# Loading the first seven row tiles for the norms into a buffer of the weight conversions

## The chip, the cores and the metric

The kernel runs on one core of a Trainium2 chip. The metric is the device time in microseconds, the median of several runs. The engines are named as the profile names them: PE is TensorE, which multiplies matrices, and PEld its weight load; DVE is VectorE; ACT is ScalarE; POOL is GpSimd; SP is SyncE, which in this kernel only issues transfers (DMAs). A `q` behind an engine's name (SPq) is the queue of transfers that this engine issues.

## The reference, cut to what matters

Attention with positive random features, and a gated feed-forward layer behind it, all in float32:

```python
# q, k, v: (8, 8, 576, 64); omega: (128, 64)
def phi(x):
    proj = np.einsum('bhsd,md->bhsm', x, omega)
    sq = np.sum(x * x, axis=-1, keepdims=True) / 2.0
    h = proj - sq
    h = h - np.max(h, axis=-1, keepdims=True)
    return np.exp(h) / np.sqrt(m)
q_p, k_p = phi(q * scale), phi(k * scale)
kv  = np.einsum('bhsm,bhsd->bhmd', k_p, v)
z   = np.sum(k_p, axis=2)
out = np.einsum('bhsm,bhmd->bhsd', q_p, kv) / (np.einsum('bhsm,bhm->bhs', q_p, z)[..., None] + 1e-06)
# x: (4608, 512), the heads side by side
y = (1 / (1 + np.exp(-(x @ w_gate))) * (x @ w_val)) @ w_out
```

The weights come as float64: they are converted on the chip. `sq`, the sum of the squares of each row of q and k in each head, is what this document calls the norms.

## The kernel before, in words

The 8 batches are worked as four units `u` of two batches, so a unit has 1152 rows, nine tiles of 128 rows. Each unit falls into two halves `b`, because of the batch limit in the middle of the fifth tile, and into four pairs of heads `p`.

Work is written as Python generators that are stepped in turn. `attention` (L681) keeps up to six of them active and takes one step of each in turn: for each unit and half one `norms` task for k and one for q (one norms task at a time), four `keys` tasks (two at a time) and four `queries` tasks. The first unit starts with the first two key tasks and the norms of k; the norms of q follow when those of k are done.

- `norms` (L493): for each row tile it loads 128 rows of all heads (128 x 512, 256 KB, L499) into a tile `nat`, of which there are three, squares it on ACT into `x2` (L501), and sums each head's 64 squares on DVE into `ss` (L503). When all tiles of the half are through, one small DVE instruction scales the sums into `sq` (L507). In the first half of a unit k has five row tiles and q four; in the second half it is the other way about.
- `projected` (L513): loads k or q the other way round (`raw`, L519), waits until `sq` of its unit and half is there, splits each group of row tiles into a high part (ACT, L70) and a low part (POOL, L71), and multiplies both by omega in three matmuls each (PE, L547 to L549, the result in `pp`). DVE takes the maximum (L552) and joins it with `sq` (L556).
- `keys` (L561): loads v (L571), works out the bias `nb` (DVE, L574), takes the exponent of each tile and head (ACT, L587), multiplies by v (PE, L595, `pkv`) and copies the result out (ACT, L600, `kv`). One key task has ten exponents, which are computed tile by tile with both heads in turn, while the matmuls go through all five tiles of the first head and then of the second. A product of this line shows as two matmuls in the trace, so one task has twenty.
- `queries` (L604) follows with transposes, exponents and products, and stores x, transposed, to memory.

Beside that, weights are converted: `first_weights` (L153) takes the four tiles `e0` to `e3`, `convert_weights` (L166) fourteen tiles `c0` to `c13`. Each is a tile of 128 x 3584 words with the tag `cv`, of which there are two: four parts take the raw float64 words (two loads of 512 KB, L144), two the result, one is scratch. A conversion is six DVE instructions (L78 to L94) and one POOL instruction (L96) for each half. A step of `first_weights` is taken with every 32nd step of the attention (L725). When the first 256 columns of x are through, the first pass of the feed-forward layer (`gv`, L247) is mixed in; later come the second pass (`gw`, L351) and the output product (`po`, L465).

A tile with a tag and a number of buffers waits for the tile that used its buffer before: the fourth `nat` load waits until the first `nat` has been squared, and so on. The order of the instructions in each engine's list is fixed when the program is built, from the order of the code and from when a planner takes each to be ready; on the chip each list runs in order, so an instruction that waits holds up all that stand behind it in its list. That counts for SP's list of transfers too.

Of the kernel before, what the change touches and what calls it, by code (L numbers as in the profile page):

```python
# [9 lines left out]
F32 = mybir.dt.float32  # L10
# [4 lines left out]
U32 = mybir.dt.uint32  # L15
# [3 lines left out]
DM = H * D  # L19
DF = 1536  # L20
P = 128
# [21 lines left out]
WP = 512  # L43
# [56 lines left out]
def attn_glu_kernel(ctx: ExitStack, tc, qT, kT, qn, kn, va, om, ident, w, out):  # L100
# [382 lines left out]
        yield  # L483

    sqs, kvs, kmid = {}, {}, {}
    through = [0] * NP

    def span(name, b):

        g = GROUPS[name][b]  # L490
        return g[0][0], g[-1][-1] + 1

    def norms(pool, name, u, b, src):  # L493

        t0, t1 = span(name, b)
        s = pool.tile([P, MID + 1, H], F32, tag="ss", bufs=2, name=f"ss{name}{u}_{b}")[:, : t1 - t0]
        for t in range(t0, t1):
            x = pool.tile([P, DM], F32, tag="nat", bufs=3, name=f"nat{name}{u}_{t}")
            nc.sync.dma_start(out=x, in_=src[u, :, t, :])  # L499
            x2 = pool.tile([P, DM], F32, tag="x2", bufs=2, name=f"x2{name}{u}_{t}")  # L500
            nc.scalar.activation(out=x2, in_=x, func=AF.Square)  # L501
            yield
            nc.vector.tensor_reduce(  # L503
                out=s[:, t - t0, :], in_=x2.rearrange("p (h d) -> p h d", d=D), axis=AX.X, op=ALU.add
            )
        sq = pool.tile([P, MID + 1, H], F32, tag="sq", bufs=6, name=f"sq{name}{u}_{b}")
        nc.vector.tensor_scalar(  # L507
            out=sq[:, : t1 - t0], in0=s, scalar1=SCALE * SCALE / 2.0, scalar2=None, op0=ALU.mult
        )
        sqs[name, u, b] = sq  # L510
        yield
# [158 lines left out]
    for u in range(U):  # L670
        for b in range(2):
            for n, x in (("k", kn), ("q", qn)):
                for p in range(NP):
                    if p == 1:
                        tasks.append((("n" + n, u, b), (), lambda pool, a=(n, u, b, x): norms(pool, *a)))
                    needs = (("k", u, p, b - 1),) if n == "k" and b else (("k", u, p, b), ("q", u - 1 + b, p, 1 - b)) if n == "q" else ()
                    make = keys if n == "k" else queries
                    tasks.append(((n, u, p, b), needs, lambda pool, a=(u, p, b), f=make: f(pool, *a)))
# [32 lines left out]
    with tc.tile_pool(name="early", bufs=1) as early:  # L711
        gates = first_pass()
        with tc.tile_pool(name="a", bufs=1, side="right") as pool:
# [7 lines left out]
            n = 0  # L721
# [7 lines left out]
            n = credit = 0  # L729
# [16 lines left out]
        for n, _ in enumerate(gates):  # L746
# [6 lines left out]
            if n == left - 2 * NE:  # L753
                parts = operands(0)
                x = next(parts)
# [110 lines left out]
```

## Time and profile before

| | us |
|---|---|
| median of 3 runs | 1237.84 (1237.4 to 1239.83) |
| the profiled execution, its own time | 1239.43 |
| span of the profile | 1237.6 |
| mean granted TensorE clock | 0.968 |

| engine | busy us | share of the span |
|---|---|---|
| PE | 1172.3 | 95% |
| DVE | 864.5 | 70% |
| POOL | 542.7 | 44% |
| ACT | 530.7 | 43% |

Row of a timeline: start in us from the start of the span, duration in us, engine, line of the code, operation, output tile <- input tiles, shapes, how many instructions are merged in the row, and in square brackets how long the engine had been idle before and what released it. Transfers stand there with the time at which SP issued them, not with the time at which the data landed. Row of a view by windows: the stretch, its length, the busy time of each engine with the number of its instructions, the granted TensorE clock (1.00 is full speed), the busy share of the 16 DMA engines and the rate. Row of a view of transfers: name, queue, number, size, and the median time in us from issue to landing.

The attention with the weight conversions and the first pass fills the first 590 us; after that PE runs the second pass and the output product almost without a gap.

### The profile page before, as it was taken

The page shows a single profiled execution, that of the slowest core. Times are in us where ns is not written, and L with a number is a line of the kernel's source. Part 1 is how long each engine was busy: PE and PEld are TensorE (multiplying, and loading weights), DVE is VectorE, ACT ScalarE, POOL GpSimd, SP SyncE. Part 2 cuts the span into 40 slices and gives each one's busy share as a digit, 9 for nine tenths or more (in the row PEclk, how much of TensorE's full clock was granted, in tenths as well). Part 3 has the DMA queues.
Part 4 walks back from the last instruction along what each step waited for, and adds up shares of the span by engine and source line. Part 5 has one row for each costly group of instructions (what it writes and reads, how often), then busy time and mean ns, then how long its engine had stood idle before and what let it go on. Part 6 is the DMA issues. An engine that isn't in the chain of part 4 may idle for free.

```text
span 1237.6 us, 23990 instructions
## 1 busy us (share of the span) xinstructions
PE 1172.3 (95%) x8828; PEld 1109.8 (90%) x8828; DVE 864.5 (70%) x1907; ACT 530.7 (43%) x1164; POOL 542.7 (44%) x599
## 2 busy tenths in 40 slices
PE   6798989999898999899899999999998899999998
PEld 5788978798887888788899999999998899999998
DVE  4889888999698866433566656666569777777773
ACT  5556755565455463342423322232325344343331
POOL 2454365556457552131466666666666211111110
PEclk7798989999899999899899999999999999999999
DMA  7667767786657641461432333323337676666662
GB/s 247 213 199 228 210 219 253 238 268 237 226 182 252 223 153 39 139 202 52 152 128 106 123 135 124 121 93 125 124 135 267 203 226 195 188 191 189 198 191 94
DMA packets 104950, 219.43 MB, mean 177 GB/s; under 512 B 11136, under 2 KB 42112, under 8 KB 103040
## 3 DMA queue, kind: packets, MB, share of 16 engines
q1 hardware_dynamic: 87984, 198.94, 48.5%
q10 hardware_dynamic: 16848, 18.95, 4.4%
q8 instruction: 70, 1.15, 0.4%
q14 instruction: 48, 0.39, 0.1%
HBM read 141.82 MB, written 76.02 MB: 176 GB/s over the span
## 4 chain that ended last, share of the span: by engine, by line
PE 71%; DVE 12%; issue 7%; DMA 5%; POOL 3%; ACT 1%; SPq 1%; ACTq 0%; DVEq 0%; POOLq 0%
PE gw L351 27%; PE po L465 20%; PE gv L247 10%; PE pkv L595 4%; PE pnq L638 4%; PE ptq L626 2%; DVE mxq L552 2%; DVE hq L615 1%; DMA xr<-xT 1%; DMA xT<-xsq 1%; DMA rawk<-kT 1%; POOL loq L71 1%; DVE hmq L556 1%; PE ppk L547 1%; POOL xe L71 1%
## 5 line engine op out<-in xcount | busy, mean ns | idle before, releaser
L351 PE MATMUL gw<-xl,u 128*128 128x256 f32 x3024 | 364.6, 283 | 6.9 <-ACT p L362 3.6
L351 PEld LDWEIGHTS gw<-xl,u 128*128 128x128 f32 x3024 | 363.5, 191 | 7.9 <-DVE u L331 3.9
L465 PE MATMUL po<-u,yh 128*128 128x256 f32 x1512 | 272.4, 283 | 0.0
L465 PEld LDWEIGHTS po<-u,yh 128*128 128x128 f32 x1512 | 234.8, 191 | 0.0
L465 PE MATMUL po<-u,yl 128*128 128x256 f32 x756 | 214.0, 283 | 3.3 <-DVE yl L71 3.3
L247 PE MATMUL gv<-xe,wh 128*128 128x512 f32 (+1 forms) x640 | 201.0, 388 | 2.1 <-POOL xe L71 2.1
L70 ACT ACTIVATE yh<-yr 128x896 fp32r<-128x896 f32 x108 | 100.2, 950 | 156.8 <-PE po L465 86.3
L465 PEld LDWEIGHTS po<-u,yl 128*128 128x128 f32 x756 | 144.3, 191 | 3.9 <-DVE yl L71 3.9
L247 PEld LDWEIGHTS gv<-xe,wh 128*128 128x128 f32 x640 | 117.3, 194 | 20.1 <-POOL xe L71 4.5
L71 POOL TENSOR_TENSOR yl<-yr,yh 128x896 fp32r<-128x896 f32 x17 | 38.0, 2232 | 215.3 <-PE po L465 139.9
L247 PE MATMUL gv<-xe,wl 128*128 128x512 f32 (+1 forms) x320 | 125.8, 394 | 2.7 <-POOL wl L71 1.6
L71 DVE TENSOR_TENSOR yl<-yr,yh 128x896 fp32r<-128x896 f32 x91 | 103.0, 1144 | 31.5 <-PE po L465 19.1
L331 DVE TENSOR_TENSOR u<-gw,p 128x256 f32<-128x256 f32 x144 | 60.7, 422 | 59.2 <-PE gw L351 51.1
L595 PE MATMUL pkv<-v,kpk 128*128 128x66 f32 x512 | 84.4, 290 | 13.3 <-ACT kpk L587 12.6
L595 PEld LDWEIGHTS pkv<-v,kpk 128*128 128x128 f32 x512 | 77.0, 209 | 21.5 <-ACT kpk L587 19.8
L71 POOL TENSOR_TENSOR lok<-rawk,hik 128x256 fp32r<-128x256 f32 (+1 forms) x80 | 55.5, 712 | 68.0 <-ACT hik L70 67.6
L456 DVE TENSOR_TENSOR yr<-yr 128x128 f32<-128x128 f32 x144 | 60.1, 451 | 35.3 <-DMA yr<-ye 34.8
L71 POOL TENSOR_TENSOR xe<-xr,xe 128x512 fp32r<-128x512 f32 (+1 forms) x40 | 49.1, 1244 | 74.2 <-ACT xe L70 62.4
L71 POOL TENSOR_TENSOR loq<-rawq,hiq 128x256 fp32r<-128x256 f32 (+1 forms) x80 | 56.5, 718 | 55.5 <-ACT hiq L70 54.7
L587 ACT ACTIVATE kpk<-ppk,nb 128x128 f32<-128x128 f32 x256 | 69.8, 393 | 17.4 <-DVE nb L574 17.1
L638 PEld LDWEIGHTS pnq<-kv,qpq 128*128 128x128 f32 (+1 forms) x640 | 70.5, 189 | 6.5 <-ACT qpq L628 4.3
L638 PE MATMUL pnq<-kv,qpq 128*128 128x66 f32 (+1 forms) x640 | 74.9, 273 | 1.4 <-ACT qpq L628 1.2
(108 smaller groups left out, 2166.6 us busy)
## 6 DMA issues: line engine op xcount, KB each, us to landing
yl<-yl SPq DMA_DIRECT2D x36, 896.0 KB, 3.8
yr<-yl SPq DMA_DIRECT2D x72, 448.0 KB, 3.5
xr<-xT SPq DMA_DIRECT2D x68, 256.0 KB, 4.7
c<-w SPq DMA_DIRECT2D x28, 512.0 KB, 5.1
w<-c SPq DMA_DIRECT2D x14, 1024.0 KB, 4.5
v<-va SPq DMA_DIRECT2D x32, 330.0 KB, 3.4
natk<-kn SPq DMA_DIRECT2D x36, 256.0 KB, 4.2
natq<-qn SPq DMA_DIRECT2D x36, 256.0 KB, 3.9
```

Of the source, the lines that this page charges most:

```text
L70: nc.scalar.activation(out=hi, in_=x, func=AF.Copy)
L71: (lo_engine or nc.vector).tensor_tensor(out=lo, in0=x, in1=hi.bitcast(F32), op=ALU.subtract)
L247: nc.tensor.matmul(gv, lhsT=u[:, s], rhs=v, start=(m == 0), stop=(m == 3 * KC - 1))
L331: return nc.vector.tensor_tensor(out=o, in0=a, in1=b, op=ALU.add)
L351: nc.tensor.matmul(o, lhsT=u[:, k, s], rhs=v[:, kc, :], start=(first and m == 0), stop=(m == 5), skip_group_check=not first,)
L456: nc.vector.tensor_tensor(out=raw[:, o], in0=raw[:, a], in1=raw[:, b], op=op)
L465: nc.tensor.matmul(o, lhsT=u[:, i, :], rhs=v[:, k, :], start=(j + m == 0 and n in (1, 6, 5, 4)), stop=(j == NPAIR - 1 and m == 2), skip_gr ...
L552: nc.vector.tensor_reduce(out=m.rearrange("p t h -> p (t h)"), in_=pp, axis=AX.X, op=ALU.max)
L587: nc.scalar.activation(out=kp[t][:, h, :], in_=pp[:, 2 * i + h, :], func=AF.Exp, bias=nb[:, t - t0, h : h + 1], scale=SCALE,)
L595: nc.tensor.matmul(pkv[:, h, :], lhsT=kp[b * MID + i][:, h, :], rhs=v[:, i, h, :], start=(i == 0), stop=(i == MID),)
L626: nc.tensor.transpose(out=pt[:, i, :], in_=h_sb[:, i, :], identity=id_sb)
L638: nc.tensor.matmul(pn[r, 2 * i + h, :], lhsT=qp[:, 2 * i + h, r], rhs=kvs[u, p, bb][:, h, :], start=True, stop=True,)
```

## The change

The first seven loads of `norms` (the five k tiles and the first two q tiles of the first half of the first unit) go to seven parts, of 2 KB in each partition, of one tile of the tag `cv`, which has just room for seven. So none of them waits for a `nat` buffer to come free. All later row tiles use the three `nat` buffers as before. Since that tile takes the first of the two `cv` buffers, `e0` takes the second and `e1` the first, once the seven tiles in it have been squared; before, `e0` and `e1` found both free.

```diff
     sqs, kvs, kmid = {}, {}, {}
+    firsts = []
     through = [0] * NP
...
         for t in range(t0, t1):
-            x = pool.tile([P, DM], F32, tag="nat", bufs=3, name=f"nat{name}{u}_{t}")
+            if not firsts:
+                firsts.append(pool.tile([P, 7 * WP], U32, tag="cv", bufs=2, name="nats").bitcast(F32))
+            if u == 0 and b == 0 and len(firsts) < 8:
+                n = len(firsts) - 1
+                firsts.append(firsts[0][:, n * DM : (n + 1) * DM])
+                x = firsts[-1]
+            else:
+                x = pool.tile([P, DM], F32, tag="nat", bufs=3, name=f"nat{name}{u}_{t}")
             nc.sync.dma_start(out=x, in_=src[u, :, t, :])
```

## The prediction

> **What bounds the kernel now.** I read the page first, then, since the change touches only the first 16 us, the timeline of each engine there, the landing times of the transfers, and the windows for rate and clock.
>
> ```profile
> span 1237.6 us, 23990 instructions
> PE   6798989999898999899899999999998899999998
> PEclk7798989999899999899899999999999999999999
> ```
>
> Each digit is a fortieth of the span, 30.9 us. PE is the bound nearly everywhere, but its first digit is 6 and the clock granted to it there 7: the opening is a chain of waits, and it is the only stretch that the change can shorten directly. From the 20th digit on PE is full, so what the attention saves earlier comes off the end.
>
> SP's list in the opening (start, duration, how many are merged), then landing times of single row tiles, v and the first q tiles (last number: us from issue to landing):
>
> ```profile
> 1.65 0.42 SPq L499 DMA_DIRECT2D natk<-kn x1
> 2.58 4.83 SPq L499 DMA_DIRECT2D natk<-kn x3
> 7.46 0.43 SPq L571 DMA_DIRECT2D v<-va x1
> 8.69 0.33 SPq L499 DMA_DIRECT2D natk<-kn x1
> 9.06 0.43 SPq L571 DMA_DIRECT2D v<-va x1
> 9.59 4.31 SPq L499 DMA_DIRECT2D natq<-qn x3
> 16.32 0.91 SPq L144 DMA_DIRECT2D e<-w x2
> ```
>
> ```profile
> natk<-kn SPq DMA_DIRECT2D x1, 256.0 KB, 5.3
> ```
>
> ```profile
> v<-va SPq DMA_DIRECT2D x1, 330.0 KB, 3.3
> natk<-kn SPq DMA_DIRECT2D x1, 256.0 KB, 2.8
> ```
>
> ```profile
> natk<-kn SPq DMA_DIRECT2D x1, 256.0 KB, 4.1
> ```
>
> ```profile
> natq<-qn SPq DMA_DIRECT2D x3, 256.0 KB, 4.4
> ```
>
> The row at 2.58 holds three issues in 4.83 us; one alone takes 0.42. So two went out at once and the fourth row tile only near 7.1, when the first had been squared; the fifth went out at 8.69, and three q tiles needed 4.31 us. Landing is issue plus the last number: the third k tile about 3.0 + 5.3 = 8.3, the fourth 7.1 + 2.8 = 9.9, the fifth 8.69 + 4.1 = 12.8.
>
> What those landings hold up, on ACT, DVE and PE:
>
> ```profile
> 12.91 0.63 ACT L501 ACTIVATE x2k<-natk 128x512 f32<-128x512 f32 x1 [2.10 <-DMA natk<-kn]
> 14.44 1.28 ACT L501 ACTIVATE x2q<-natq 128x512 f32<-128x512 f32 x2 [0.90 <-DMA natq<-qn]
> 16.66 2.18 ACT L587 ACTIVATE kpk<-ppk,nb 128x128 f32<-128x128 f32 x8 [0.95 <-DVE nb L574]
> 19.18 2.24 ACT L587 ACTIVATE kpk<-ppk,nb 128x128 f32<-128x128 f32 x8
> 26.28 0.28 ACT L600 ACTIVATE kv<-pkv 128x132 f32<-128x132 f32 x1 [2.95 <-PE pkv L595]
> 26.46 1.52 ACT L70 ACTIVATE hik<-rawk 128x256 fp32r<-128x256 f32 x5
> ```
>
> ```profile
> 10.65 0.69 DVE L503 TENSOR_REDUCE ssk<-x2k 128x8 f32<-128x512 f32 x1 [0.44 <-ACT x2k L501]
> 13.57 0.69 DVE L503 TENSOR_REDUCE ssk<-x2k 128x8 f32<-128x512 f32 x1 [1.64 <-ACT x2k L501]
> 14.18 0.68 DVE L552 TENSOR_REDUCE mxk<-ppk 128x4 f32<-128x512 f32 x1
> 15.87 0.68 DVE L552 TENSOR_REDUCE mxk<-ppk 128x4 f32<-128x512 f32 x1
> 16.47 0.16 DVE L574 SCALAR_TENSOR_TENSOR nb<-sqk,hmk 128x10 f32<-128x10 f32 x1
> 22.45 0.43 DVE L78 TENSOR_SCALAR e<-e 128x512 uint32<-128x512 uint32 x1 [4.15 <-DMA e<-w]
> ```
>
> ```profile
> 8.49 0.58 PE L547 MATMUL ppk<-omH,lok 128*128 128x256 f32 x1 [8.49 <-POOL lok L71]
> 14.21 0.41 PE L549 MATMUL ppk<-omH,hik 128*128 128x256 f32 x1
> 14.79 0.28 PE L549 MATMUL ppk<-omH,hik 128*128 128x256 f32 x1
> 17.08 2.25 PE L595 MATMUL pkv<-v,kpk 128*128 128x66 f32 x8 [2.01 <-ACT kpk L587]
> 27.72 0.58 PE L547 MATMUL ppk<-omH,lok 128*128 128x256 f32 x1 [1.48 <-POOL lok L71]
> ```
>
> The fifth k tile lands at 12.8, its square ends at 13.54, its sum at 14.26, and only behind that does DVE get to the maximum at 14.18, to two more and to that of 15.87; the bias of the first key task (16.47) follows, its exponents start at 16.66, and PE, done with projections at 14.79 + 0.28 = 15.07, starts again at 17.08 after 2.01 us without work. Everything behind hangs on it in order: the second kv at 26.28, the next split at 26.46, the next projection at 27.72.
>
> **The change part by part.** *SP.* SP issued the first three tiles 0.47 apart (1.65, then 2.58 with one transfer between). Without the waits the fourth and fifth go out at about 3.5 and 4.0. v, v and the three q tiles follow at that pace from 4.4 to 6.3 instead of 7.46 to 13.9. No instruction is added, no transfer either; the byte count is the same.
>
> *Landing.* What had been held back by SP now stands behind other bytes:
>
> ```profile
> 6.00:8.00 2.00, 0.00 (x0) 0.00 (x0) 0.69 (x1) 1.41 (x4) 0.28 (x1) 1.00 0.65 250
> 8.00:10.00 2.00, 1.51 (x7) 1.51 (x8) 1.17 (x2) 1.81 (x6) 2.00 (x4) 1.00 0.87 287
> 10.00:12.00 2.00, 2.00 (x11) 2.00 (x11) 1.49 (x3) 0.81 (x2) 1.35 (x3) 1.00 0.89 262
> 12.00:14.00 2.00, 2.00 (x12) 2.00 (x11) 0.43 (x1) 0.63 (x1) 0.00 (x0) 1.00 0.81 302
> ```
>
> The last two numbers are the DMA engines' share and GB/s. The transfers are nearly busy already, 250 to 302 GB/s, with only 0.65 at 6 to 8. A tile of 256 KB (0.262 MB) takes 0.262 / 0.27 = 1.0 us at such a rate, so behind the third tile (8.3) the fourth lands at 9.3 and the fifth at 10.3. Bounds: 9.3 if the rate has slack, 12.8 if the bytes set it and nothing moves; I take 10.3, since row tiles so far landed in the order of issue, and the share of 0.65 leaves room. Then v, v and two q tiles, 2 x 0.338 + 2 x 0.262 = 1.2 MB at 282 (mean of the last two rows) need 4.25 us: the second q tile lands at 14.5, and its square ends at 14.5 + 0.64 = 15.15. ACT has both q squares ahead of the exponents (14.44, then 16.66).
>
> *The bias.* The sum of the fifth k tile now ends at about 10.3 + 0.63 + 0.69 = 11.6, say 12.2 with a maximum in between; it is late no more. Late next is PE's projection: the maximum of the row 15.87 needs the matmul that starts at 14.21 and ends at 14.62, and DVE's list has it ahead of the bias, although it belongs to the second key task. So that maximum runs from 14.65 to 15.25, where it ran from 15.87 to 16.47, and the exponents start at 15.45 (16.66 less 1.22), just behind the q squares' 15.15. **Gain 1.2 us**: 2.6 us earlier norms are worth less than half, since the projection and the q squares come next.
>
> *Clock and the products behind.* PE's gap shrinks from 2.01 to about 0.8 us. What the clock makes of that:
>
> ```profile
> 14.65:18.06 3.41, 1.29 (x7) 1.00 0.93 291
> 21.47:24.89 3.42, 3.42 (x18) 0.50 1.00 385
> ```
>
> (Stretch, length, PE busy, clock, DMA share, rate.) A stretch of 3.41 us with 1.29 us of work was followed by half speed, and a stretch full of `pkv`, 18 in 3.42 us, 0.19 us each, stayed at half. So a busy PE is not enough: these short products do not bring the speed back. In the changed kernel the stretch to 18.06 holds two projections and some ten products that wait for exponents; I take half speed from 18.06 as now, and the gain stays 1.2 us. The Trainium skill ("TensorE: Matmul & The Clock Gate", the table of the two states) has the clock fall only after at least one idle window of about 3.4 us; the trace disagrees, since it fell here after an idle time of 2.01 us. By this page of the Trainium skill the smaller gap would leave full speed; what this gives is the rival below.
>
> *The buffers.* e0 moves to the other `cv` buffer and costs nothing. e1 waits for the second q square, about 15.2, and today e0 itself is issued only at 16.32, with e1 behind it: nothing. If the code called for e1 earlier, it would wait on SP with all loads behind it; that cover is the 16.32. In the later rotation every tile waits for the same predecessor as before: e2 for e0, as now. The `nat` rotation likewise, save for the first tiles of the next half, which find free buffers.
>
> *e0's load.* It stands ten issues of 0.47 behind the fifth k tile's 4.0, plus 0.5, so it may go out at 9.2 instead of 16.32. With the same bytes ahead of it, it lands at best the slack of the DMA engines earlier: (1 - 0.65) x 2.0 + (1 - 0.81) x 2.0 = 1.1 us. DVE waited 4.15 us for it and had time; nothing.
>
> Sum against the profiled execution (1239.43, span 1237.6): 1.2 us off, a span of 1236.4. The median of the runs is 1.6 below that execution, so the forecast is 1237.84 - 1.2 = **1236.6**. A shift of the opening also moves all work against the clock's steps of 3.41 us: a stretch more or less at half speed costs up to 1.7 us, and one or two of those either way make the scatter of this case, 1236.6 within 2.6.
>
> **The rivals.** *The clock stays up* (or DVE's list is put in another order, with the first bias ahead of the second task's maximum, so that the products begin at 15.07 and are dense). Then the second task's first pass ends with its exponents, 15.45 + 2 x 2.52 (the distance of 16.66 and 19.18) = 20.5, and ten products at half of 0.19 end at 21.5; the second kv comes 4.8 us earlier than 26.28: **1233.0**. For: the gap is less than half. Against: the two rows above, full of such products and still at half. 0.20.
>
> *e0's conversion stands ahead of the first bias* (slower). DVE's list is made anew, and e0's load moves up seven us in SP's. If its first DVE step (22.45, which waits for the landing) comes to stand before the bias, the exponents start at 22.45 + 0.43 + 0.16 = 23.0 instead of 16.66, 6.4 later: **1244.2**. It decides from the point where that one step passes the bias; standing behind it, it costs nothing. For: e0 does move up, and the list is not just the code's order (a load of v stands at 7.46 ahead of the fifth k tile). Against: today both biases and two sums stand between. 0.14.
>
> *The bytes bind and nothing gets earlier*: the fifth tile still lands near 12.8, or the second q tile, only now behind both v, lands as late as today, and its square holds the exponents. Gain about 0: **1237.8**. For: shares of 0.87 and 0.89. Against: the 0.65. 0.16.
>
> **How the numbers follow.** The forecast has 0.50. A measurement of this kernel can tell about 0.2% (2.5 us; three runs spread over 2.4). Faster by more: 0.16 of the forecast's own scatter, 0.19 of the clock rival, 0.03 of the bytes rival, 0.38. Slower: 0.03 of the forecast, 0.13 of e0's rival, 0.03 of the bytes', 0.19. Within: the rest, 0.43. The range goes from 1231.0, the clock rival with one more stretch at full speed, to 1241.5, the forecast's scatter and the lower side of e0's; most of e0's case (0.12) and the lowest of the clock's (0.06) are left out.
>
> **What would show it.** In SP's list five row tiles in a row by 4.5 us, with no wait; the fifth k square near 10.4 rather than 12.91; the first exponent near 15.4; PE's gap under 1 us; second kv near 25. Wrong: a first exponent before 14 or after 16.6, full speed from 18 to 25, or DVE waiting for e0 ahead of the first bias. If the opening gains 1.2 and the end does not, the gain was given back later.

## The result, and the profile after

| | before | after |
|---|---|---|
| median of 11 runs, us | 1239.37 (1232.04 to 1242.72) | 1245.34 (1242.12 to 1252.72) |
| ratio, 95% interval | | **1.0066** (1.0047 to 1.0084) |
| the profiled execution, its own time | 1239.43 | 1245.34 |
| its span | 1237.6 | 1243.5 |

The change made the kernel 0.7% slower (by the two medians 6 us are lost, by the ratio 8), where 1.2 us were forecast as won. Lines of `after` stand 8 higher than the same lines of before (L501 is now L509, L587 is L595, L600 is L608).

From the page of the kernel after, the busy time in 40 slices of 31.1 us and the granted clock:

```profile
span 1243.5 us, 24005 instructions
PE   5888899899898989899999999999998899999998
PEclk9699999999799999999999999999999999999999
```

The clock's first digit has gone from 7 to 9, so the opening runs better than before. The loss hardly shows at this grain: PE has a few more eights among its nines up to the 17th digit. It takes positions in the work and windows to find it.

**The opening.** SP's list of the kernel after, then ACT, DVE and PE (start, duration, how many):

```profile
2.58 1.90 SPq L507 DMA_DIRECT2D nats<-kn x4
4.53 1.25 SPq L579 DMA_DIRECT2D v<-va x2
```

```profile
9.96 1.17 ACT L509 ACTIVATE x2k<-nats 128x512 f32<-128x512 f32 x2
12.66 1.28 ACT L509 ACTIVATE x2q<-nats 128x512 f32<-128x512 f32 x2 [1.33 <-DVE sqk L515]
14.44 2.17 ACT L595 ACTIVATE kpk<-ppk,nb 128x128 f32<-128x128 f32 x8 [0.50 <-DVE nb L582]
21.09 0.28 ACT L608 ACTIVATE kv<-pkv 128x132 f32<-128x132 f32 x1 [0.18 <-PE pkv L603]
```

```profile
8.96 2.93 DVE L511 TENSOR_REDUCE ssk<-x2k 128x8 f32<-128x512 f32 x4 [0.93 <-ACT x2k L509]
14.25 0.16 DVE L582 SCALAR_TENSOR_TENSOR nb<-sqk,hmk 128x10 f32<-128x10 f32 x1
14.44 1.02 DVE L560 TENSOR_REDUCE mxk<-ppk 128x4 f32<-128x512 f32 x2
```

```profile
14.47 0.28 PE L557 MATMUL ppk<-omH,hik 128*128 128x256 f32 x1
14.86 1.98 PE L603 MATMUL pkv<-v,kpk 128*128 128x66 f32 x8
```

```profile
18.00:20.00 2.00, 1.92 (x18) 1.78 (x16) 0.00 (x0) 2.00 (x9) 0.00 (x0) 1.00 0.84 280
```

All five k tiles are issued by 4.5 us with no wait. DVE takes four sums in a row and has the first bias (14.25) *ahead* of the second task's second maximum (14.44); before, that maximum (15.87) stood ahead of the bias (16.47). So exponents start at 14.44 (before 16.66), PE goes over from projections (14.47 + 0.28 = 14.75) to products at 14.86, the clock stays at 1.00 from 18 to 20, and the second `kv` copy comes at 21.09 instead of 26.28: 5.2 us won. e0's first conversion step is at 21.02, behind both biases.

**Behind the opening.** Below, the start of some of ACT's 32 `kv` copies, of the first `gw` and of the last `po` product: for before the time, for the others the difference to it, each from one profiled execution. The kernels e1 to h2 are those of the experiments.

| | before | after | e1 | g1 | g2 | h1 | i1 | h2 |
|---|---|---|---|---|---|---|---|---|
| 2nd kv | 26.28 | -5.19 | -1.27 | -4.33 | -3.62 | -5.41 | -0.07 | -5.37 |
| 11th | 155.06 | -4.85 | -1.26 | -2.25 | +2.08 | -5.48 | +2.57 | -2.56 |
| 16th | 225.65 | -6.28 | -3.95 | +1.37 | -0.60 | -4.35 | +2.64 | -2.39 |
| 19th | 281.65 | -2.78 | -3.90 | +2.07 | +2.25 | -0.59 | +2.72 | -2.33 |
| 23rd | 344.28 | -0.78 | -3.88 | +1.75 | +4.09 | -6.31 | -5.01 | -9.91 |
| 27th | 407.30 | +4.11 | -4.10 | +1.16 | +8.71 | -1.99 | -5.25 | -8.54 |
| 32nd | 467.04 | +8.73 | -4.18 | +1.01 | +13.24 | +1.32 | -5.41 | -8.79 |
| first gw | 585.34 | +7.16 | -4.06 | -1.72 | +13.19 | -0.27 | -6.71 | -11.49 |
| last po | 1232.63 | +5.82 | -5.64 | -4.81 | +11.76 | -3.51 | -6.57 | -12.25 |

Between 226 and 467 us the kernel after loses 8.73 + 6.28 = 15.0 us. Its windows row of that stretch (PE's busy time first, the clock third from the end):

```profile
225.00:470.00 245.00, 223.39 (x1545) 198.26 (x1545) 200.75 (x497) 126.94 (x352) 130.22 (x152) 0.95 0.63 211
```

and that of the kernel before:

```profile
225.00:470.00 245.00, 231.02 (x1624) 203.39 (x1623) 205.22 (x516) 134.43 (x373) 141.01 (x164) 0.98 0.64 215
```

PE is busy 7.6 us less and its clock is 0.03 lower, 0.03 x 225 = 6.8 us: together 14.4 of the 15.0. The work is the same. What differs is the order: the kernel has 1279 entries in ACT's list, 1907 in DVE's, 579 in SP's, 595 in POOL's and 8188 in PE's, and 478, 712, 157, 79 and 1351 places of them hold another instruction than before, the opening's and those of hundreds of us later. The longest waits of PE in that stretch, in the timeline of the kernel after (in brackets the idle time and what ended it):

```profile
235.71 0.44 PE L663 MATMUL pxq<-id_sb,xq 128*128 128x128 f32 x1 [2.65 <-DVE xq L657]
319.26 0.48 PE L603 MATMUL pkv<-v,kpk 128*128 128x66 f32 x1 [3.96 <-ACT kpk L595]
392.61 0.55 PE L555 MATMUL ppq<-omH,loq 128*128 128x256 f32 x1 [2.40 <-ACT xsq L669]
460.75 0.43 PE L603 MATMUL pkv<-v,kpk 128*128 128x66 f32 x1 [2.81 <-ACT kpk L595]
```

### The profile page after: what moved, and what is told of

Same layout as the page of the kernel before. It is cut to its first block, busy times and chain, and to the rows that moved or that the text cites. A ratio compares the mean times of both kernels' runs of the same rounds, so it can differ in the third digit from the quotient of the medians.

```text
span 1243.5 us, 24005 instructions
## 1 busy us (share of the span) xinstructions
PE 1167.5 (94%) x8828; PEld 1106.2 (89%) x8828; DVE 869.7 (70%) x1907; ACT 528.4 (42%) x1164; POOL 544.0 (44%) x599
## 4 chain that ended last, share of the span: by engine, by line
PE 70%; DVE 14%; issue 6%; DMA 5%; POOL 3%; ACT 1%; SPq 1%; ACTq 0%; DVEq 0%; POOLq 0%
PE gw L351 27%; PE po L465 20%; PE gv L247 10%; PE pkv L603 5%; PE pnq L646 3%; DMA xT<-xsq 2%; DVE mxq L560 2%; PE ptq L634 1%; DVE mxk L560 1%; DVE hq L623 1%; POOL loq L71 1%; DVE hmq L564 1%; PE pxq L663 1%; PE ppk L555 1%; DVE c L88 1%
## 5 line engine op out<-in xcount | busy, mean ns | idle before, releaser
L71 DVE TENSOR_TENSOR yl<-yr,yh 128x896 fp32r<-128x896 f32 x91 | 98.5, 1100 | 28.9 <-ACT yh L70 11.7
L456 DVE TENSOR_TENSOR yr<-yr 128x128 f32<-128x128 f32 x144 | 63.8, 476 | 38.8 <-DMA yr<-ye 38.2
L595 ACT ACTIVATE kpk<-ppk,nb 128x128 f32<-128x128 f32 x256 | 69.6, 391 | 17.5 <-DVE nb L582 16.8
```

What stands on the lines that cost most here:

```text
L71: (lo_engine or nc.vector).tensor_tensor(out=lo, in0=x, in1=hi.bitcast(F32), op=ALU.subtract)
L456: nc.vector.tensor_tensor(out=raw[:, o], in0=raw[:, a], in1=raw[:, b], op=op)
L595: nc.scalar.activation(out=kp[t][:, h, :], in_=pp[:, 2 * i + h, :], func=AF.Exp, bias=nb[:, t - t0, h : h + 1], scale=SCALE,)
```

## The experiments

**The theories.** *Lists*: the shared buffer does what was forecast; the planner remade every engine's list for it, and the remade lists lose behind the opening. *Buffer*: the shared buffer, or the earlier opening, itself costs something later. To tell them apart, both sets of lists are read from builds without and with the shared buffer, and the final program is built with each engine held to a chosen list:

```diff
+    old, new = lists_of(*build(False)), lists_of(*build(True))
+    nc, _ = build(shared, lists)
...
+def impose(tc, traced, lists):
+    for engine in lists.values():
+        for a, b in zip(engine, engine[1:]):
+            tc.add_manual_dep(traced[b], traced[a].name, order, reason="list")
```

The second line is the one in which the experiments differ: its first argument says whether the shared buffer is used, the second which lists are held. Each time below is a median, each ratio (with its 95% interval) is to runs of the kernel before on the same chip, whose medians were 1237.0 to 1239.3.

### e1: the shared buffer with the lists of before

```diff
+    nc, _ = build(True, old)
```

> The seven loads go to the shared buffer as in the changed kernel, but every engine's list of instructions is held to the order of the kernel before. The lists theory (the new buffers gain about 5 us in the opening, and the remade lists lose 12 us between 240 and 480 us): second kv near 21 to 25 us instead of 26.3, and the end 2 to 5 us earlier than the kernel before, ratio 0.996 to 0.999. The buffers theory (the early loads or the shifted rotation of the two conversion buffers slow the conversions later, in whatever order): about as slow as the changed kernel, ratio 1.004 to 1.008. The chance theory (any shift of the opening falls otherwise against the clock's steps and is worth plus or minus some us by chance): a ratio on either side, with the loss not in the stretch from 240 to 480.

1233.58 us, **0.9965** (0.9946 to 0.9983). ACT's timeline of e1:

```profile
11.10 0.63 ACT L509 ACTIVATE x2k<-nats 128x512 f32<-128x512 f32 x1 [0.49 <-DMA nats<-kn]
12.64 1.30 ACT L509 ACTIVATE x2q<-nats 128x512 f32<-128x512 f32 x2 [0.91 <-DMA nats<-qn]
15.39 2.18 ACT L595 ACTIVATE kpk<-ppk,nb 128x128 f32<-128x128 f32 x8 [1.44 <-DVE nb L582]
25.00 0.28 ACT L608 ACTIVATE kv<-pkv 128x132 f32<-128x132 f32 x1 [2.95 <-PE pkv L603]
```

and windows rows of e1, of the opening and of the long stretch:

```profile
18.00:20.00 2.00, 2.00 (x10) 2.00 (x11) 0.43 (x1) 2.00 (x10) 0.00 (x0) 0.50 0.79 312
225.00:470.00 245.00, 230.91 (x1639) 203.61 (x1639) 202.90 (x518) 133.45 (x373) 137.00 (x160) 0.98 0.63 212
```

This is the forecast's opening nearly to the digit (how nearly is partly luck, as g2 shows): exponents at 15.39 (forecast 15.45), half speed from 18 on, second `kv` 1.27 us earlier (forecast 1.2). What held the exponents is the projection that the forecast named, in DVE's and PE's timelines of e1:

```profile
14.59 0.69 DVE L560 TENSOR_REDUCE mxk<-ppk 128x4 f32<-128x512 f32 x1 [0.45 <-PE ppk L557]
15.81 1.99 PE L603 MATMUL pkv<-v,kpk 128*128 128x66 f32 x8 [0.89 <-ACT kpk L595]
```

From 226 to 467 us the difference to before stays (-3.95, -4.18). The buffer costs nothing later. That e1 wins another 2.7 us between the 11th and the 16th `kv` was not forecast and stays open.

### e2: the three buffers of before with the remade lists

```diff
-    nc, _ = build(True, old)
+    nc, _ = build(False, new)
```

> Three nat buffers as in the kernel before, but every engine's list held to the order of the changed kernel. The lists theory: the opening loses its gain (second kv back near 25 to 26 us) and the loss from 240 to 480 us stays, so 8 to 12 us slower than the kernel before, ratio 1.006 to 1.010. The buffers theory: as the kernel before, ratio 0.999 to 1.002.

1251.49 us, **1.0113** (1.0088 to 1.0138). The lists alone lose, a little more than the range expected, and more than with the buffer, for which they were made.

### g1 and g2: the sets of lists joined at 45 us

At about 45 us both sets have done the same instructions on every engine, so they can be joined there without a seam. g1 takes the remade lists for the opening and those of before behind it, g2 the other way round:

```diff
-    nc, _ = build(True, old)
+    nc, _ = build(True, joined(new, old, {"Activation": 51, "SP": 31, "DVE": 48, "Pool": 35, "PE": 168}))
```

> The shared buffer with each engine's list of the changed kernel up to about 45 us and the lists of before from there on. At this place both sets of lists have done the same set of instructions on each engine, so no list has a seam. Lists theory (the remade lists lose after 230 us, the opening only gains): the second kv about 5.2 us early as in the changed kernel, the shift held to the end as with the lists of before, ratio 0.994 to 0.997, about 1232 to 1235. Rival (what the opening saves is lost later whatever the lists behind it are, because work runs ahead of its transfers or weights): early to 155 us, then given back, ratio about 1.00 or above.

> The shared buffer with each engine's list of before up to about 45 us and the lists of the changed kernel from there on; again no seam. Lists theory: first exponents at 15.4 and the second kv 1.3 us early as with the lists of before, then loses 10 to 13 us between 230 and 470 us: ratio 1.008 to 1.012, about 1249. Rival (the remade lists lose only because the opening runs 5 us ahead): no loss, ratio about 0.997.

g1: 1234.4 us, **0.9952** (0.993 to 0.9975). g2: 1248.35 us, **1.0086** (1.0053 to 1.0118). As the lists theory had it: the loss goes with the lists behind 45 us, whichever the opening. The opening of g2 was not as expected: with the lists and buffers that e1 has there, its exponents start at 14.25 and the second `kv` comes 3.6 us early, not 1.3. In g2 PE's projections start 0.12 us apart from 11.3 us on, in e1 0.21 us apart until 14.5, so what the bias waits for is ready earlier; e5, with the same opening, is like g2 (from 11.4 us on, second `kv` 3.3 us early). Single steps are less tidy: in its profile g1 loses 3.6 us between 155 and 226 us that h2, with the same entries there, does not; so a position read from one execution can be some 4 us off. The waits of PE are steadier. The four shown above (2.65, 3.96, 2.40 and 2.81 us in the kernel after) are there in g2 (2.67, 4.12, 1.64 and 2.76) and in e2 (2.67, 4.00, 1.77 and 2.77), both with remade lists behind 45 us; e1 and g1, with the lists of before there, have only the second (2.62 and 2.31), as the kernel before has (2.47).

### e3, e5 and f1: joins with a seam

e3 changes from the remade lists to those of before near 299 us, e5 from those of before to the remade ones near 240; f1 has remade lists, SP's excepted.

```diff
-    nc, _ = build(True, old)
+    nc, _ = build(True, joined(new, old, {"Activation": 491, "SP": 196, "DVE": 525, "Pool": 177, "PE": 1477}))
...
+    nc, _ = build(True, joined(old, new, {"Activation": 388, "SP": 163, "DVE": 411, "Pool": 141, "PE": 1143}))
...
+    nc, _ = build(True, {**new, "SP": old["SP"]})
```

> Shared buffer; the lists are the changed kernel's for what runs in about the first 299 us and those of the kernel before for the rest (both hold the same instructions up to the cut). The lists theory, with a loss spread over 240 to 480: by 299 us the changed kernel was still 3 us ahead, so the end is about 3 us earlier than the kernel before, ratio 0.997 to 0.999. The buffers theory: ratio 1.004 to 1.008.

> Shared buffer; the lists of the kernel before for what runs in about the first 240 us, those of the changed kernel for the rest. The lists theory: the gain of the opening up to 240 us, then the changed kernel's loss of 12 us, so 5 to 9 us slower than the kernel before, ratio 1.004 to 1.008. If the loss grew out of the first 240 us (conversions or loads left in an unlucky state there), the old lists there cure it: ratio 0.995 to 1.000.

> Shared buffer; the lists of PE, DVE, ACT and POOL are the changed kernel's, only SP's list of transfers is that of the kernel before. If the 11 us by which the remade lists are behind come from transfers that stand too late or wait in SP's list: most comes back, ratio to the kernel before 0.997 to 1.001. If they come from the compute engines' lists: as the changed kernel, ratio 1.004 to 1.009.

e3: 1246.69 us, 1.0086 (1.0054 to 1.0118), missed. e5: 1251.09 us, 1.0106 (1.0084 to 1.0129). f1: 1270.32 us, 1.0298 (1.0265 to 1.033), far outside both of its ranges. e5 too is above the range that it had from the lists theory, and e3 by itself would fit the buffer theory better. At 299 and 240 us the engines' lists could be joined only each for itself, at slightly different times. SP's timeline of e3 shows the price:

```profile
263.21 0.42 SPq L144 DMA_DIRECT2D c<-w x1
273.39 0.33 SPq L280 DMA_DIRECT2D ye<-ye x1
274.25 1.39 SPq L507 DMA_DIRECT2D natq<-qn x3
```

```profile
270.00:280.00 10.00, 4.35 (x29) 3.35 (x28) 7.65 (x19) 1.38 (x4) 6.52 (x9) 0.96 0.51 162
```

SP waits ten us with a store, the q tiles stand behind it, and PE works 4.35 of 10 us. f1's 25 us above the kernel after are probably of the same kind, a list being worth something only with the other lists for which it was made; f1's trace was not taken apart. By their times these three decide nothing, and g1 and g2 replaced them. By positions behind the seam they agree with the theory: from the 21st to the 32nd `kv` e3, on the lists of before, goes from 7.3 to 6.6 us behind the kernel before, and e5, on the remade ones, from 6.6 to 15.7. New lists of ACT, DVE or PE singly were not tried.

### e4 and f5: five tiles shared, and one

```diff
-            if u == 0 and b == 0 and len(firsts) < 8:
+            if u == 0 and b == 0 and len(firsts) < 2:
```

(one tile; 6 for five), with the planner's own lists.

> Only the five k tiles go to the shared buffer, the two q tiles to the nat buffers; the planner makes the lists. By the lists theory the direct gain is the same 1 to 5 us of the opening, and the planner makes yet other lists: anywhere from 1229 to 1251, most likely not within 2 us of the changed kernel. By the buffers theory it is as slow as the changed kernel, ratio 1.004 to 1.008.

> Only the first k tile is loaded into the shared buffer and everything else as before, with the lists that the planner makes for that. It takes away one wait for a buffer, so by itself it can win at most about the 1.3 us that the shared buffer won with the lists of before. Lists theory: whatever it does beyond that comes from the lists that the planner makes anew, so the time can stand 5 to 15 us off that of before while the opening moves by 1.3 us or less; on either side. Rival (the sharing of seven tiles is what costs): within 2 us of before, ratio 0.998 to 1.001.

e4: 1247.25 us, **1.010** (1.007 to 1.013). f5: 1234.6 us, **0.9974** (0.9952 to 0.9996). The traces say why: apart from the names of the buffers, ACT, DVE, SP and POOL go through the same order in f5 as in before, and in e4 the same as in the kernel after. One tile in the shared buffer wins the opening's 1.29 us and leaves the plan alone; five tip it into the other one. So f5 is also a control for e1: the same lists, made by the planner and not imposed, come out alike (0.9974 and 0.9965). And e4 has the four waits of PE again (2.67, 3.94, 1.80 and 2.73 us). That the time would move by 5 to 15 us with every such edit was wrong: here there are two plans, and an edit lands on one.

### f2 and f3: no round trip of x

In the kernel after, two of the four waits of PE shown above (319 and 392 us) come behind an ACT entry that waits for x to be loaded for the feed-forward layer (`xr`), which in turn waits for the store of x (`xT`); the one at 461 us comes behind a copy of x that waits for an older store. f2 (remade lists) and f3 (lists of before) load `xr` from the transposed keys instead, so that the feed-forward part computes on other data:

```diff
-            nc.sync.dma_start(out=raw[:, k], in_=xT[k, :, o : o + n])
+            nc.sync.dma_start(out=raw[:, k], in_=kT[0, k, :, o % NC : o % NC + n])
```

> Shared buffer and the changed kernel's lists, but the feed-forward layer loads its x from an input of the same size instead of from the attention's result in memory, so these loads wait for no store (the feed-forward part thus computes on other data). The round-trip theory (in the remade ACT list the split of the loaded x stands ahead of exponents and copies, which then wait for the store of x to land and for the load behind it; the PE gaps at 319 and 392 us end that way): 4 to 8 us faster than the changed kernel, and the distance to the same edit with the old lists shrinks from 11 us to under 6. The other theory (many small misplacements in the lists of ACT, DVE and PE): within 3 us of the changed kernel, and 8 to 12 us behind the same edit with the old lists.

> The same edit with the shared buffer and the lists of the kernel before: the control. Both theories: 0 to 3 us faster than the shared buffer with the old lists alone, so ratio to the kernel before 0.993 to 0.997.

f2: 1233.7 us, **0.9987** (0.9956 to 1.0018). f3: 1242.02 us, **1.0052** (1.0026 to 1.0077): against what was expected, slower than e1, from which it takes a wait away. Both lose 15 to 16 us between the 4th and the 11th `kv` (47 to 155 us), at a clock of 0.73 and 0.78 in 45 to 95 us where e1 has 0.90; why, stays open. Only from the 11th `kv` to the first `gw` do they fit the theory: with the remade lists the round trip makes the difference between losing 12.0 us (after) and winning 6.8 (f2), with the lists of before it makes none (winning 2.8 and 2.1). By the whole time they decide nothing.

### h1: four entries of ACT's remade list moved

ACT's timeline at the longest wait, in the kernel after:

```profile
311.80 1.09 ACT L636 ACTIVATE qpq<-ptq 128x512 f32<-128x512 f32 x2
318.32 0.63 ACT L70 ACTIVATE xe<-xr 128x512 fp32r<-128x512 f32 x1 [5.44 <-DMA xr<-xT]
318.86 2.15 ACT L595 ACTIVATE kpk<-ppk,nb 128x128 f32<-128x128 f32 x8
```

Eight exponents, which PE waits for, stand behind a split of x that waits 5.44 us for its load; their bias was through on DVE at 312.6:

```profile
311.93 0.69 DVE L582 SCALAR_TENSOR_TENSOR nb<-sqk,hmk 128x8 f32<-128x8 f32 x1
```

h1 moves this entry and three more behind what they hold up:

```diff
+    act = lists["Activation"]
+    for n, to in ((560, 568), (671, 674), (778, 785), (776, 784)):
+        act.insert(to, act.pop(n))
```

> The changed kernel with its own remade lists, but four of ACT's 1279 entries each put behind the instructions that they held up: two splits of x (xe, which waited 5.44 us at 318.32 and 2.54 us at 391.57 for a load of x) go behind eight exponents and behind one q split, and one copy of x with its store (460.05, which waited 1.16 us for the store before it) goes behind eight exponents. Theory (the remade lists lose because an instruction that waits for the round trip of x through memory stands in ACT's list ahead of work that PE needs): the PE gaps of 3.96, 2.40 and 2.81 us at 319, 392 and 461 us shrink to under 1 us, 6 to 9 us come off, ratio 0.999 to 1.002. Rival (the gaps only show where PE waits; whatever is taken away there comes back at the next wait, since another engine or the clock sets the pace): at most 3 us off, ratio 1.004 to 1.007.

1235.64 us, **0.9984** (0.9957 to 1.0012), some 10 us under the kernel after. The same place in h1:

```profile
314.04 1.09 ACT L636 ACTIVATE qpq<-ptq 128x512 f32<-128x512 f32 x2
315.01 2.17 ACT L595 ACTIVATE kpk<-ppk,nb 128x128 f32<-128x128 f32 x8
320.51 0.63 ACT L70 ACTIVATE xe<-xr 128x512 fp32r<-128x512 f32 x1 [3.32 <-DMA xr<-xT]
```

The exponents run at once; the split still waits, and costs nothing. The Trainium skill ("TensorE: Matmul & The Clock Gate", the section on architectural detail) calls ACT's queue strictly first in, first out; the two traces agree: behind the waiting split the exponents started at 318.86, 6.2 us after their bias, ahead of it at 315.01.

Of the gain 7.0 us come between the 19th and 21st `kv` (after -2.78 to -0.30, h1 -0.59 to -5.08), 1.9 between the 29th and 31st (461 us), and 0.6 between the 23rd and 27th (392 us). At 392 us PE's wait is gone in h1, but h1 still loses 4.3 us there, nearly as much as the kernel after (4.9), so most of that loss has another cause, which was not found. The gain at the first place is not yet the theory's loss either: **the lists of before have the same order at the first place**, and a wait of PE there too. In e1:

```profile
317.38 0.33 PE L603 MATMUL pkv<-v,kpk 128*128 128x66 f32 x1 [2.62 <-ACT kpk L595]
```

### h2 and i1: the same entry moved in the lists of before

h2 is g1 with this one entry moved; i1 is the kernel before, with its own three buffers and its own lists, and the same move.

```diff
+    for n, to in ((561, 569),):
+        act.insert(to, act.pop(n))
```

> The joined lists (opening of the changed kernel to about 45 us, then those of before) with one entry of ACT moved: the split of x ahead of the PE gap of 2.31 us at 322.83 goes behind the eight exponents that follow it. Theory: that gap goes, 2 us come off against the joined lists alone, ratio about 0.993 to 0.994. Rival (the wait comes back elsewhere): as the joined lists alone, 0.995 to 0.997.

> The kernel before, its own three buffers and its own lists, with one of ACT's 1279 entries moved: the split of x that waits 3.73 us at 319.88 for its load goes behind the eight exponents that follow it. Theory (such an entry costs the PE gap that it makes, 2.47 us at 320.82, and the slow clock behind that gap, 0.59 in 320 to 330 and 0.89 in 330 to 340, some 5 us): 7 us off, whatever the buffers are, ratio 0.993 to 0.995. Rival (the gain of the same move in the joined lists came from the earlier opening): 2 us or less, ratio 0.998 to 1.000.

h2: 1226.11 us, **0.9912** (0.988 to 0.9945), the lowest ratio of all. i1: 1229.86 us, **0.9939** (0.9919 to 0.996). The windows of the kernel before around its wait of 2.47 us (320.82):

```profile
310.00:320.00 10.00, 7.62 (x52) 6.41 (x50) 8.82 (x26) 4.52 (x12) 4.50 (x6) 1.00 1.02 365
320.00:330.00 10.00, 9.18 (x46) 9.00 (x47) 2.17 (x10) 3.66 (x12) 1.26 (x1) 0.59 0.36 120
330.00:340.00 10.00, 9.80 (x60) 8.48 (x59) 8.29 (x18) 4.97 (x19) 7.39 (x10) 0.89 0.54 193
```

and of i1:

```profile
310.00:320.00 10.00, 9.37 (x68) 8.24 (x66) 10.00 (x27) 6.02 (x16) 5.53 (x7) 1.00 1.01 357
320.00:330.00 10.00, 10.00 (x86) 9.66 (x85) 7.01 (x22) 4.76 (x16) 3.53 (x4) 1.00 0.78 263
330.00:340.00 10.00, 9.86 (x74) 8.98 (x73) 9.23 (x21) 7.15 (x26) 6.72 (x9) 1.00 0.61 204
```

The wait costs itself, 2.5 us, and the slow clock behind it, 10 x 0.41 + 10 x 0.11 = 5.2: 7.7 together. In the table i1 gains 2.72 + 5.01 = 7.7 from the 19th to the 23rd `kv`. h2 came out lower than expected (0.993 to 0.994, which its interval still reaches); the expectation priced the wait and left out the clock.

### i2: the third place in full

At the third place (461 us in the kernel after) PE still waited 2.29 us in h1, since an older copy of x, which waits for the store before it, stood ahead of the exponents as well:

```profile
453.02 0.38 ACT L669 ACTIVATE xsq<-pxq 128x256 f32<-128x256 f32 x1 [3.06 <-DMA xT<-xsq]
454.74 0.44 PE L603 MATMUL pkv<-v,kpk 128*128 128x66 f32 x2 [2.29 <-ACT kpk L595]
```

i2 moves it too, with its store and a split:

```diff
+    for n, to in (..., (775, 783), (774, 782), (772, 781)):
```

> The changed kernel with its remade lists and the four moved entries, and three more moved at the third place: the copy of x that waited 3.06 us for the store before it, its store and a split of x go behind the eight exponents too, whose bias was ready 3 us before they started. Theory: the PE gap of 2.29 us that was left at 455 goes, 2 to 3 us come off against four moved entries, ratio 0.996 to 0.997. Rival (the wait comes back at the next use of x): as with four, 0.998 to 0.999.

1232.19 us, **0.9959** (0.9937 to 0.998). The wait is gone and from the 29th to the 31st `kv` i2 loses 0.5 us where h1 loses 2.9. The two intervals overlap; the profile at the place is the better evidence. Between the 23rd and the 27th `kv` i2 loses 5.0 us, as the kernel after does.

## Why the prediction was wrong

- **SP, and the landings**: right as far as the fifth k tile. Five tiles are out by 4.5 us; the fifth lands 4.02 + 6.2 = 10.2 in the kernel after (forecast 10.3), and at 4.49 + 6.5 = 11.0 in e1, where a v stands ahead of it. As forecast, it no longer holds up the bias. Two terms behind it were mis-sized, at no cost, since nothing on the way to the bias waited for them. The bytes did not set the pace at 282 GB/s: with SP's waits gone the transfers reached 390, and the second q square ended at 13.94 (forecast 15.15). So a share of 0.81 to 0.89 in the kernel before was not yet full. And SP did not keep the pace of 0.47 us: the third q tile went out at 8.15 (forecast 6.3) and e0 at 12.59 (forecast 9.2). From 6.67 to 13.91 each issue comes within 0.03 us of the landing of the transfer eight places ahead of it in SP's list. SP's timeline and a windows row of the kernel after:

```profile
8.15 0.33 SPq L507 DMA_DIRECT2D natq<-qn x1
12.59 0.98 SPq L144 DMA_DIRECT2D e<-w x2
```

```profile
12.00:14.00 2.00, 2.00 (x12) 2.00 (x12) 1.97 (x6) 1.26 (x2) 0.00 (x0) 1.00 1.04 390
```

- **The bias, PE's gap, the clock**: right for the list that the prediction read. With it (e1) exponents start at 15.39, PE waits 0.89 us, half speed comes and 1.27 us are won. That the size fits to 0.1 us is partly luck: the end of the projections was read from one execution, and with the same opening g2 and e5 won 3.6 and 3.3 us, since their projections became faster some 3 us earlier. But the kernel after does not have that list. In it the first bias stands ahead of the second task's second maximum, the case that the prediction put in brackets at the clock rival: products are dense from 14.86, the clock stays, and 5.2 us are won where that rival had 4.8. The prediction's reading that such products do not bring the speed back holds only where a gap came first; without one they kept it.
- **e0's conversion ahead of the bias** and **bytes bind**: neither happened. e0 was converted at 21.02; the tiles came earlier.
- **The step that failed**: "From the 20th digit on PE is full, so what the attention saves earlier comes off the end", with all lists behind the opening taken as they were. It had the fact in hand (the lists are made anew when the program is built, and the DVE list was named as a risk for one conversion) and priced it for the first 25 us only. The remade lists lose 15.0 us between 226 and 467 us, through waits of PE and the slow clock behind them. The prediction's last sign, that the gain was "given back later", came true, but it had no price there. With the lists of before behind 45 us, the forecast's direction comes back: e1 0.9965, g1 0.9952. Its size does so only within a few us: e1's interval, 2 to 7 us, lies above the 1.2 forecast. e2 shows the lists losing without the buffer and without the faster opening, g2 with the lists of before up to 45 us.
- **The scatter of 2.6 us** was worked out from clock steps alone; a second plan that differs by 12 us (after against e1) was outside it.

What is shown: the loss comes with the remade lists behind 45 us; at one place in both plans, and at 461 us in the remade one, an ACT entry that waits for x ahead of ready exponents makes PE wait and lose its clock. What is not is more than half of the 15.0 us: 3.5 of them are lost between the 16th and the 19th `kv`, around the wait at 235 us, where `xq` stands on DVE behind work that runs with hardly a gap from 230.78 on, and 4.9 between the 23rd and the 27th; the moves of h1 and i2 leave both. That these two were faster than the kernel after by some 10 and 13 us comes to more than half from the first place, which cost the kernel before time as well. Open too are why the planner prefers the second order, and the 15 us of f2 and f3.

## What to carry to other kernels

Where a planner orders the instructions, the first thing to compare after an edit is the order of each engine's list, over the whole program: a small edit in the opening put other instructions in over a third of ACT's and DVE's places, and that outweighed the edit's own gain (hold the lists to separate the two). An entry that waits for a round trip through memory belongs behind whatever in its list is ready and feeds the engine that bounds the kernel. Price a wait of that engine with the slow clock that may follow it, not by its length alone.

## What the runs showed of the hardware

A wait of PE of 2.47 us was followed by a clock of 0.59 over the next 10 us and so cost three times its length; behind 3.96 us in the kernel after, and behind 0.89 us in the opening of e1 (PE busy 2.79 of the 4 us from 14 to 18), the clock was 0.50. With 0.11 us between projections and products in the kernel after (busy 3.58 of the same 4 us) it stayed at 1.00, and so it did in e1 around a wait of 1.84 us at 384 us (windows row of e1):

```profile
380.00:390.00 10.00, 6.93 (x47) 5.79 (x47) 7.48 (x20) 5.27 (x18) 6.82 (x10) 1.00 0.92 283
```

The Trainium skill ("TensorE: Matmul & The Clock Gate", the section on why this matters for kernels) advises against idle gaps above about 3 us; in these traces shorter ones were enough in some places and not in others, and no run here shows what decides. The time from which PE's projections in the opening start 0.12 us apart instead of 0.21 differs from profile to profile, 11.3 us in g2 and 14.5 us in e1, and that moved the second `kv` by more than 2 us. The other surprise is how far one order of a list is bound to the others: f1, with SP's list of one plan and the other engines' lists of the second, took 25 us more than the kernel after.
